# A dense layer's first matrix by one level of Strassen, its activations through DRAM

## Chip, cores and metric

The kernel runs on one core of a Trainium2 chip. The metric is the device time of one launch in microseconds (us), lower is better; it is given as the median of three runs. The trace is that of one profiled execution.

## What is computed

Attention between 8 batches of rows and 32 state rows, a top-1 mixture of 8 experts over the 4352 resulting rows of 512 features, and a dense layer over the same rows. The change lies in the dense layer, the last third of the reference:

```python
def _moe2_ref(x, w_in, w_out):          # x 4352 x 512, w_in 512 x 2048, w_out 2048 x 512
    h = x @ w_in
    beta = 1.0
    neg = h <= -beta
    pos = h >= beta
    g = np.where(pos, h, np.where(neg, 0.0, (h + beta) ** 2 / (4.0 * beta)))
    return (g @ w_out).astype(np.float32)
```

The mixture hands its rows over as y, still without each row's scale (gate weight times output gate): x = scale * y.

## The kernel before

The kernel has one core's engines: TensorE (PE) for matrix products, VectorE (DVE), ScalarE (ACT), Pool for element-wise work and indirect DMAs, and SP, whose queue issues most DMAs. Everything up to the dense layer takes the first 597 us of the trace and stays as it is. One program is written and a scheduler sets each engine's order from it; buffers come from pools of a fixed number, and the tools put in the waits.

**Three passes.** A float32 operand is held as h, its rounding to the 12-bit format float32r, and l, the rest (a cast on ScalarE, a subtraction on VectorE); a product is h·h + l·h + h·l, three matmuls of the fast format that add up in one PSUM bank.

**The dense layer.** The 34 tiles of 128 tokens are worked in blocks: tiles 0 and 1, then seven blocks of four tiles, then two of two (`blocks`, L393). For a block `dense_in` (L395) loads y, transposed, in 512 x 512 (features by tokens), multiplies it by the scale (DVE, L411) and splits it (ACT L412, DVE L413). The 2048 hidden features are 16 chunks of 128. The weights of a chunk, its 512 x 128 of w_in and its 128 x 512 of w_out in one tile of 1024 columns, are split in the first block (`split_w`, L167 to L171) and stay in 32 tiles. `ff_l1` (L418) makes one chunk of h for a block: 12 matmuls (4 blocks of 128 features x 3 passes, L427) with as many columns as the block has tokens, 512 or 256. Then the function g is made of h in four steps, and the result is split for the next product (ACT L440, DVE L441):

```python
V.tensor_scalar(c[:, 0:n], p[:, 0:n], 1.0, -1.0, op0=ALU.min, op1=ALU.max)      # L434
A.activation(r[:, 0:n], p[:, 0:n], AF.Relu, bias=neg1)                          # L435
A.activation(c[:, 0:n], c[:, 0:n], AF.Square, bias=half, scale=0.5)             # L436
V.tensor_add(c[:, 0:n], c[:, 0:n], r[:, 0:n])                                   # L437
```

`ff_l2` (L461) takes a chunk of g as the stationary operand: for each tile of the block 3 matmuls of 512 columns (L470) that add to that tile's output bank; after 16 chunks `store_z` (L450) copies the bank out (ACT L453) and writes the rows to their places (Pool, indirect DMA, L454). The schedule (L1193 on) goes through all (block, chunk) steps and runs the second matrix two steps (`AHEAD`) behind the first, across the borders of blocks. So TensorE alternates between 12 matmuls of a first and of a second matrix. g never leaves the core's memory.

PSUM is cut into eight banks of 512 columns: two (`ptp`) for transposes, two (`pl1`) for h, four (`pacc`) for outputs. The pool `np_` belongs to a preparation of the weights that is over before the dense layer; `gp` has six tiles of 512 columns for short-lived values.

Of the kernel before, what the change touches and what calls it, by code (L numbers as in the profile page):

```python
# [1277 lines left out]
```

## Time and profile before

| | us |
|---|---|
| runs | 1353.61, 1356.83, 1357.52 |
| median | 1356.83 |
| span of the profiled execution | 1351.2 |
| of it up to the dense layer's first product | 597.5 |
| dense layer, block 0 (2 tiles) | 44 |
| dense layer, seven blocks of 4 tiles | 616 |
| dense layer, two blocks of 2 tiles | 87 |
| from the last product to the end | 7 |

The rows to read are those of the engines in the dense layer: how long each is busy in a stretch, how far apart TensorE's matmuls start, and how long one operation of each kind takes on VectorE, ScalarE and Pool. A matmul's own duration in the trace is longer than its place in the pipeline, since matmuls overlap; the distance between starts is what counts. PEclk is the share of full clock that TensorE was granted.

### The profile page before, as it was taken

To read this page: it belongs to the slowest core of one execution; us is meant where nothing else is said; L and a number is where in the kernel's file an instruction comes from. 1 tells how busy PE (TensorE), PEld (TensorE's weight loads), DVE (VectorE), ACT (ScalarE), POOL (GpSimd) and SP (SyncE) were. 2 spreads that over 40 slices of the span, in tenths; PEclk is the share of its full clock that TensorE was granted. 3 is DMA by queue.
4 is the path that set the end of the run, shared out by engine and by line. 5 is a ranking of instruction groups with operands and counts; after the bars stand their busy time and mean duration, and the time that the engine had idled before them with its cause. 6 is when DMAs were issued, how large, how long until landed. Compare 5 with 4: busy or idle time off the path is not lost.

```text
span 1351.2 us, 17570 instructions
## 1 busy us (share of the span) xinstructions
PE 1305.1 (97%) x6534; PEld 1081.3 (80%) x6534; DVE 706.5 (52%) x1303; ACT 579.6 (43%) x982; POOL 139.3 (10%) x146
## 2 busy tenths in 40 slices
PE   6988989989899999999999999999999999999997
PEld 3767778767887788899888888888888888888996
DVE  5787768756765535355453443534435344343443
ACT  3654256434543435355344334433344343433443
POOL 2212022122132001000001001000010010100100
PEclk8999989999999999999999999999999999999999
DMA  6976398867777546250000101001010010000100
GB/s 237 334 253 223 91 351 261 300 194 226 254 229 231 183 141 226 94 185 9 32 24 32 40 0 48 24 8 63 1 47 25 0 47 20 32 16 16 35 17 16
DMA packets 79043, 154.23 MB, mean 114 GB/s; under 512 B 12068, under 2 KB 35048, under 8 KB 78952
## 3 DMA queue, kind: packets, MB, share of 16 engines
q1 hardware_dynamic: 70952, 129.94, 29.1%
q0 software_dynamic: 8000, 23.11, 4.9%
q8 instruction: 53, 0.87, 0.3%
q14 instruction: 38, 0.31, 0.1%
HBM read 116.79 MB, written 36.23 MB: 113 GB/s over the span
## 4 chain that ended last, share of the span: by engine, by line
issue 61%; PE 16%; DMA 11%; DVE 5%; POOL 2%; ACT 2%; SPq 1%; POOLq 0%; ACTq 0%; DVEq 0%
DMA wf_dram<-n 7%; PE h L284 6%; PE y L345 4%; DMA raw<-w 3%; POOL out L454 2%; PE xp L1017 2%; PE sc L916 1%; PE sp L994 1%; DVE n L263 1%; DVE n L264 1%; PE xp L194 1%; SPq L248 1%; DMA xg<-x_dram,inv_i 1%; PE ip L614 0%; DVE n L257 0%
## 5 line engine op out<-in xcount | busy, mean ns | idle before, releaser
L435 ACT ACTIVATE cr<-fh,neg 128x512 f32<-128x512 f32 (+1 forms) x160 | 99.8, 624 | 303.5 <-DVE cr L434 303.5
L437 DVE TENSOR_TENSOR cr<-cr 128x512 f32<-128x512 f32 (+1 forms) x160 | 97.9, 612 | 182.5 <-ACT cr L436 182.5
L434 DVE TENSOR_SCALAR cr<-fh 128x512 f32<-128x512 f32 (+1 forms) x160 | 97.7, 610 | 137.3 <-PE fh L427 132.3
L441 DVE TENSOR_TENSOR gl<-cr,gh 128x512 fp32r<-128x512 f32 (+1 forms) x160 | 97.8, 611 | 96.3 <-ACT gh L440 95.7
L440 ACT CAST gh<-cr 128x512 fp32r<-128x512 f32 (+1 forms) x160 | 89.2, 557 | 108.9 <-DVE cr L437 107.8
L454 POOL DMA_INDIRECT out<-zs,row_i x34 | 33.4, 981 | 793.2 <-ACT zs L453 787.8
L436 ACT ACTIVATE cr<-cr,half 128x512 f32<-128x512 f32 (+1 forms) x160 | 103.7, 648 | 0.0
L256 ACT ACTIVATE n<-n 128x256 f32<-128x256 f32 x64 | 28.0, 437 | 103.8 <-DMA wf_dram<-n 99.8
L287 ACT ACTIVATE hh<-h 128x512 fp32r<-128x512 f32 (+2 forms) x96 | 48.4, 505 | 56.1 <-PE h L284 55.9
L288 DVE SCALAR_TENSOR_TENSOR hl<-h,hh 128x512 fp32r<-128x512 f32 (+2 forms) x96 | 55.1, 574 | 23.1 <-ACT hh L287 21.5
L176 POOL DMA_INDIRECT xg<-x_dram,inv_i x38 | 40.7, 1072 | 215.3 <-DMA yT_dram<-ys 83.8
L257 DVE TENSOR_SCALAR n<-n 128x256 f32<-128x256 f32 x64 | 18.9, 295 | 61.4 <-ACT n L256 49.1
L804 POOL DMA_INDIRECT ls_dram<-pk,cdest_i x34 | 38.1, 1119 | 109.1 <-DMA ls_dram<-pk,cdest_i 107.6
L1017 PE MATMUL xp<-sB_sb,at_sb 128*128 128x272 f32 x128 | 34.4, 417 | 3.0 <-ACT at_sb L983 2.3
L194 PE MATMUL xp<-ident,xg 128*128 128x128 f32 x144 | 22.9, 284 | 10.8 <-DMA xg<-x_dram,inv_i 6.8
L1017 PEld LDWEIGHTS xp<-sB_sb,at_sb 128*128 128x128 f32 x128 | 23.3, 195 | 10.5 <-ACT at_sb L983 2.7
L194 PEld LDWEIGHTS xp<-ident,xg 128*128 128x128 f32 x144 | 18.2, 146 | 16.3 <-issue 12.3
L345 PE MATMUL y<-hh,w_1h 128*128 128x512 f32 (+1 forms) x80 | 30.1, 376 | 0.6 <-ACT ys L310 0.5
L345 PE MATMUL y<-hh,w_7h 128*128 128x512 f32 (+1 forms) x80 | 29.8, 373 | 0.0
L345 PE MATMUL y<-hl,w_3h 128*128 128x512 f32 (+1 forms) x80 | 29.7, 371 | 0.0
L345 PE MATMUL y<-hh,w_3h 128*128 128x512 f32 (+1 forms) x80 | 29.6, 370 | 0.0
L345 PE MATMUL y<-hh,w_7l 128*128 128x512 f32 (+1 forms) x80 | 29.5, 369 | 0.0
(1642 smaller groups left out, 3794.6 us busy)
## 6 DMA issues: line engine op xcount, KB each, us to landing
raw<-w SPq DMA_DIRECT2D x80, 512.0 KB
n<-wio SPq DMA_DIRECT2D x64, 256.0 KB
yT_dram<-ys SPq DMA_DIRECT2D x36, 256.0 KB
fy<-yT_dram SPq DMA_DIRECT2D x17, 512.0 KB
xn<-xn SPq DMA_DIRECT2D x32, 260.0 KB
xT<-xT SPq DMA_DIRECT2D x32, 256.0 KB
x_dram<-xr SPq DMA_DIRECT2D x32, 256.0 KB
wf_dram<-n SPq DMA_DIRECT2D x64, 128.0 KB
```

The source lines that it names most:

```text
L194: PE.transpose(p[:, k], rows[:, k * 128:(k + 1) * 128], ident)
L284: PE.matmul(p[:, 0:n], a, b, start=(i == 0), stop=(i == len(prods) - 1))
L288: last["V"] = V.scalar_tensor_tensor(hl[:, 0:n], p[:, 0:n], 0.0, hh[:, 0:n].bitcast(F32), op0=ALU.max, op1=ALU.subtract)
L345: PE.matmul(yacc[s, k * n // KK][:, c:c + n * 128], w[:, o + k * 128:o + k * 128 + 128], h[:, 0:n * 128], **g)
L434: V.tensor_scalar(c[:, 0:n], p[:, 0:n], 1.0, -1.0, op0=ALU.min, op1=ALU.max)
L435: A.activation(r[:, 0:n], p[:, 0:n], AF.Relu, bias=neg1)
L436: A.activation(c[:, 0:n], c[:, 0:n], AF.Square, bias=half, scale=0.5)
L437: V.tensor_add(c[:, 0:n], c[:, 0:n], r[:, 0:n])
L440: A.copy(gh[:, 0:n], c[:, 0:n])
L441: V.tensor_sub(gl[:, 0:n], c[:, 0:n], gh[:, 0:n].bitcast(F32))
L454: z = G.indirect_dma_start(out=out, out_offset=bass.IndirectOffsetOnAxis(ap=row_i[:, t:t + 1], axis=0), in_=zs, in_offset=None,)
L1017: PE.matmul(xp[:, g, 0:272], at_sb[:, g, st * 128:(st + 1) * 128], sB_sb[:, b, g], start=True, stop=True,)
```

## The change

Block 0 (tiles 0 and 1) is worked as before, but for two things: its weights are split into one tile for w_in and one for w_out (each with h and l side by side, `split_ff`), and g is made by `bend`, one step of ScalarE and two of VectorE, as max(h, a · min(a, 1)) with a = relu((h + 1) / 2). 

For the other 32 tiles the first matrix is done by Strassen's scheme in the form of Winograd. A group p is 1024 tokens, cut in two halves of 512; a quad q is two chunks of 128 hidden features. With the depth of 512 cut in two halves as well, the quad's 2 x 2 outputs come from seven products of half depth (`PRODS`) in place of eight: each has two blocks of 128 features x 3 passes = 6 matmuls of 512 columns, 42 in a quad in place of 48. The operands are sums and differences: of x in `x_raw` and `x_split`, made once for a group (14 tiles of h and l), of w_in in `w_sums`, made once on Pool, split in the first group, stored to DRAM (`wv_dram`) and loaded again for the later groups (`w_next`). The products share three banks per quad (x, y from the pools `ptp`, `pl1`; z from `ptp`); a bank is read between products, and five sums and a copy on VectorE and ScalarE put the outputs together. `g_out` bends each of the four 128 x 512 pieces and stores it to DRAM, on SP's queue.

The second matrix for these tiles reads g back (`l2_load`, three buffers in the place of `np_`), splits it (`l2_split`) and runs per half group of four tiles as before. Its chunks are spent by a budget, 3.5 in a quad (`PER`) from the sixth quad on (`LAG`), 4 more at the end of a group (`GAP`), and what is left behind the last quad.

```diff
+    def split_ff(raw, nm):
+        got = []
+        for part, c in (("i", 0), ("o", 512)):
+            if part == "i":
+                wi_pools.append(wstate["n"] % NW)
+            t = w_tile(F32R, f"{nm}{part}").rearrange("p (a f) -> p a f", a=2)
+            A.copy(t[:, 0], raw[:, c:c + 512])
+            V.tensor_sub(t[:, 1], raw[:, c:c + 512], t[:, 0].bitcast(F32))
+            got.append(t)
+        return got
...
-    blocks = [(0, 2)] + [(2 + 4 * i, 4) for i in range(7)] + [(30, 2), (32, 2)]
+    blocks = [(0, 2)]
+    NPAIR = (NT - 2) // 8
...
+    def bend(h, a, out):
+        A.activation(a, h, AF.Relu, bias=half, scale=0.5)
+        V.scalar_tensor_tensor(a, a, 1.0, a, op0=ALU.min, op1=ALU.mult)
+        V.tensor_tensor(out, h, a, op=ALU.max)
...
-        V.tensor_scalar(c[:, 0:n], p[:, 0:n], 1.0, -1.0, op0=ALU.min, op1=ALU.max)
-        A.activation(r[:, 0:n], p[:, 0:n], AF.Relu, bias=neg1)
-        A.activation(c[:, 0:n], c[:, 0:n], AF.Square, bias=half, scale=0.5)
-        V.tensor_add(c[:, 0:n], c[:, 0:n], r[:, 0:n])
+        c = gp.tile([128, 512], F32, tag="g", name=f"cr{j}_{fc}")[:, 0:n]
+        bend(p[:, 0:n], c, c)
...
+    PRODS = [("11", "11"), ("S2", "T2"), ("S1", "T1"), ("12", "21"), ("S3", "T3"), ("22", "T4"), ("S4", "22")]
...
+    def x_raw(p):
+        t0 = 256 + 1024 * p
+        sv = late_tile(spool, ns_, f"sv{p}", F32)
+        SP.dma_start(
+            sv, s_dram.rearrange("(o t) p -> o (t p)", o=1)[:, t0:t0 + 1024].to_broadcast([128, 1024]),
+        )
+        got = []
+        for k in (0, 1):
+            raws = []
+            for kk in (k, k + 2):
+                r = raw_tile(f"xr{p}_{kk}")
+                SP.dma_start(r, yT_dram[:, kk, t0:t0 + 1024])
+                G.tensor_mul(r, r, sv)
+                raws.append(r)
+            b11, b12, b21, b22 = [r[:, c:c + 512] for r in raws for c in (0, 512)]
+            t3 = gp.tile([128, 512], F32, tag="g", name=f"t3_{p}_{k}")
+            V.tensor_sub(t3, b22, b12)
+            V.tensor_sub(b12, b12, b11)
+            got.append({"11": b11, "T2": b11, "21": b21, "T3": t3, "T1": b12, "T4": b21, "22": b22})
+        return got
+    def x_split(p, k, nm, got):
+        v = got[k][nm]
+        if nm == "T2":
+            V.tensor_add(v, got[k]["T3"], v)
+        elif nm == "T4":
+            V.tensor_sub(v, v, got[k]["T2"])
+        t = late_tile(xpool, nx_, f"X{p}_{nm}_{k}", F32R).rearrange("p (a f) -> p a f", a=2)
+        A.copy(t[:, 0], v)
+        V.tensor_sub(t[:, 1], v, t[:, 0].bitcast(F32))
+        X[p, nm, k] = t
...
+        raw, u = [raw_tile(nm) for nm in (f"wr{q}", f"ws{q}")]
+        for j in range(2):
+            SP.dma_start(raw[:, j * 512:j * 512 + 512], wf_dram[2 * q + j][:, 0:512])
+        a11, a12, a21, a22 = [raw[:, c:c + 256] for c in range(0, 1024, 256)]
+        s1, s2, s3, s4 = [u[:, c:c + 256] for c in range(0, 1024, 256)]
+        G.tensor_add(s1, a21, a22)
+        G.tensor_sub(s2, s1, a11)
+        G.tensor_sub(s3, a11, a21)
+        G.tensor_sub(s4, a12, s2)
+        wsum[q] = {"11": a11, "S2": s2, "12": a12, "S3": s3, "S1": s1, "22": a22, "S4": s4}
...
+    def w_next(p, q, i):
+        if q == NQ2:
+            p, q = p + 1, 0
+        if p == NPAIR:
+            return
+        nm, m, j = PRODS[i][0], q // 2, q % 2
+        if j == 0:
+            W[i] = late_tile(wpool, nw_, f"W{p}_{m}_{nm}", F32R)
+            if p:
+                SP.dma_start(W[i].bitcast(F32), wv_dram[m][i])
+        if p == 0:
+            w = W[i].rearrange("p (a j f) -> p a j f", a=2, j=2)
+            v = wsum[q][nm]
+            A.copy(w[:, 0, j], v)
+            V.tensor_sub(w[:, 1, j], v, w[:, 0, j].bitcast(F32))
+            if j:
+                SP.dma_start(wv_dram[m][i], W[i].bitcast(F32))
...
+        g = gip.tile([128, 512], F32, tag="r", name=f"gi{p}_{t}_{fc}")
+        SP.dma_start(g, g_dram[p, t, fc])
...
+        g = gin.pop(c)
+        gh = hp_.tile([128, 512], F32R, tag="gh", name=f"gh{p}_{t}_{fc}")
+        gl = hp_.tile([128, 512], F32R, tag="gl", name=f"gl{p}_{t}_{fc}")
+        A.copy(gh, g)
+        V.tensor_sub(gl, g, gh.bitcast(F32))
...
+    def l2():
+        c = done["mm"]
+        for what, ahead, f in (("load", 4, l2_load), ("split", 2, l2_split)):
+            while done[what] < min(c + ahead, len(chunks)):
+                f()
...
+    def product(p, q, i, bank, start):
+        nm = PRODS[i][1]
+        w = W[i].rearrange("p (a j k f) -> p a j k f", a=2, j=2, k=2)[:, :, q % 2]
+        n = 0
+        for k in range(2):
+            x = X[p, nm, k]
+            for a, b in ((0, 0), (1, 0), (0, 1)):
+                PE.matmul(
+                    bank, w[:, a, k], x[:, b], start=(start and n == 0), stop=(n == 5), skip_group_check=True,
+                )
+                n += 1
+    def g_out(p, q, r, c, h, a):
+        bend(h, a, a)
+        g_dram[p, c, 2 * q + r] = dram.tile([128, 512], F32, name=f"g{p}_{c}_{2 * q + r}")
+        SP.dma_start(g_dram[p, c, 2 * q + r], a)
...
+    def quad(p, q, hook, after):
+        x = ptp.tile([128, 512], F32, tag="tp", name=f"qx{p}_{q}")
+        product(p, q, 0, x, True)
+        after(0)
+        tu = late_tile(tpool, nt_, f"tu{p}_{q}", F32)
+        t, u2 = tu[:, 0:512], tu[:, 512:1024]
+        A.copy(t, x)
+        y = pl1.tile([128, 512], F32, tag="l1", name=f"qy{p}_{q}")
+        product(p, q, 1, y, True)
+        after(1)
+        V.tensor_add(u2, y, t)
+        z = ptp.tile([128, 512], F32, tag="tp", name=f"qz{p}_{q}")
+        product(p, q, 2, z, True)
+        after(2)
+        hook(0)
+        product(p, q, 3, x, False)
+        after(3)
+        g_out(p, q, 0, 0, x, a_tile(f"a11_{p}_{q}"))
+        product(p, q, 4, y, False)
+        after(4)
+        u3 = a_tile(f"u3_{p}_{q}")
+        V.tensor_add(u3, y, t)
+        hook(1)
+        product(p, q, 5, y, False)
+        after(5)
+        V.tensor_add(t, t, y)
+        V.tensor_add(u3, u3, z)
+        g_out(p, q, 1, 0, t, a_tile(f"a21_{p}_{q}"))
+        g_out(p, q, 1, 1, u3, a_tile(f"a22_{p}_{q}"))
+        hook(2)
+        product(p, q, 6, z, False)
+        after(6)
+        V.tensor_add(u2, u2, z)
+        g_out(p, q, 0, 1, u2, a_tile(f"a12_{p}_{q}"))
+        hook(3)
+        done["quad"] = p * NQ2 + q
+    LAG, PER, GAP = 5, 3.5, 4
+    budget = [0.0]
+    def spend():
+        while budget[0] >= 1 and done["mm"] < len(chunks):
+            budget[0] -= 1
+            l2()
+    w_sums(0)
+    for i in range(len(PRODS)):
+        w_next(0, 0, i)
+    vals = x_raw(0)
+    for _, nm in PRODS:
+        for k in range(2):
+            x_split(0, k, nm, vals)
+    for gq in range(NPAIR * NQ2):
+        p, q = divmod(gq, NQ2)
+        last = q == NQ2 - 1
+        if p == 0 and not last:
+            w_sums(q + 1)
+        if last and p + 1 < NPAIR:
+            vals = x_raw(p + 1)
+        def hook(n):
+            if gq >= LAG:
+                budget[0] += PER / 4
+                spend()
+        def after(i):
+            if q % 2 or p == 0:
+                w_next(p, q + 1, i)
+            if last and p + 1 < NPAIR:
+                for k in range(2):
+                    x_split(p + 1, k, PRODS[i][1], vals)
+        quad(p, q, hook, after)
+        if last:
+            budget[0] += GAP
+            spend()
+    while done["mm"] < len(chunks):
+        l2()
```

TensorE's order where block 0 ends. Before, the first chunk of the next block (fh1_0) stands between block 0's second-matrix chunks (f1h0 is the block's input, wff_0h the split weights):

```order
L470 MATMUL z0_0_7143<-wff_13h_7059,gh0_13_7459 128x512 [waits Activation_49]
L470 MATMUL z0_0_7143<-wff_13l_7060,gh0_13_7459 128x512
L470 MATMUL z0_0_7143<-wff_13h_7059,gl0_13_7460 128x512 [waits DVE_49]
L470 MATMUL z0_1_7147<-wff_13h_7059,gh0_13_7459 128x512
L470 MATMUL z0_1_7147<-wff_13l_7060,gh0_13_7459 128x512
L470 MATMUL z0_1_7147<-wff_13h_7059,gl0_13_7460 128x512
L427 MATMUL fh1_0_7525<-f1h0_7137,wff_0h_5349 128x512 [waits Activation_49]
L427 MATMUL fh1_0_7525<-f1h0_7137,wff_0l_5350 128x512
L427 MATMUL fh1_0_7525<-f1l0_7139,wff_0h_5349 128x512
L427 MATMUL fh1_0_7525<-f1h0_7137,wff_0h_5349 128x512
L427 MATMUL fh1_0_7525<-f1h0_7137,wff_0l_5350 128x512
```

After, the first quads stand there alone, behind the rest of block 0. The names: qx0_1 is bank x of group 0, quad 1; X0_T4_0 the operand T4 of group 0, feature block 0; W0_0_S3 the weight operand S3 of group 0 for quads 0 and 1; x3 stands for three matmuls:

```order
L1353 MATMUL qy0_0_7688<-X0_T3_0_7648,W0_0_S3_7593 128x512 [waits DVE_49]
L1353 MATMUL qy0_0_7688<-X0_T3_0_7648,W0_0_S3_7593 128x512 x2
L1353 MATMUL qy0_0_7688<-X0_T3_1_7651,W0_0_S3_7593 128x512 x3
L1353 MATMUL qx0_1_7782<-X0_11_0_7622,W0_0_11_7581 128x512 [waits DVE_49,Activation_49]
L1353 MATMUL qx0_1_7782<-X0_11_0_7622,W0_0_11_7581 128x512 x2
L1353 MATMUL qx0_1_7782<-X0_11_1_7625,W0_0_11_7581 128x512 x3
L1353 MATMUL qy0_1_7794<-X0_T2_0_7629,W0_0_S2_7584 128x512 [waits Activation_49]
L1353 MATMUL qy0_1_7794<-X0_T2_0_7629,W0_0_S2_7584 128x512 [waits DVE_49]
L1353 MATMUL qy0_0_7688<-X0_T4_0_7655,W0_0_22_7596 128x512 [waits DVE_49]
L1353 MATMUL qy0_0_7688<-X0_T4_0_7655,W0_0_22_7596 128x512 x2
L1353 MATMUL qy0_0_7688<-X0_T4_1_7659,W0_0_22_7596 128x512 x3
L1353 MATMUL qz0_0_7699<-X0_22_0_7662,W0_0_S4_7599 128x512 [waits DVE_49]
```

The second-matrix matmuls are gone from between the products; quad 1's first product has moved ahead of quad 0's sixth (T4), and each product waits for VectorE. The first second-matrix matmul of these tiles stands 115 matmuls behind the start of quad 0.

VectorE's order at the same place. Before, three steps in each chunk:

```order
L434 TENSOR_SCALAR cr0_15_7510<-fh0_15_7497 128x256 [waits PE_49]
L437 TENSOR_TENSOR cr0_15_7510<-cr0_15_7510 128x256 [waits Activation_49]
L441 TENSOR_TENSOR gl0_15_7516<-cr0_15_7510,gh0_15_7515 128x256 [waits Activation_49]
L434 TENSOR_SCALAR cr1_0_7538<-fh1_0_7525 128x512 [waits PE_49]
L437 TENSOR_TENSOR cr1_0_7538<-cr1_0_7538 128x512 [waits Activation_49]
L441 TENSOR_TENSOR gl1_0_7544<-cr1_0_7538,gh1_0_7543 128x512 [waits Activation_49]
L434 TENSOR_SCALAR cr1_1_7566<-fh1_1_7553 128x512 [waits PE_49]
L437 TENSOR_TENSOR cr1_1_7566<-cr1_1_7566 128x512 [waits Activation_49]
```

After, the rows behind block 0's last step; t3 and xr are sums of y times scale (L1240 to L1250), X the split operands (L1253), tu the sum of banks y and x (L1378):

```order
L1248 TENSOR_TENSOR xr0_1_7613<-t3_0_1_7619,xr0_1_7613 128x512 [waits DVE_49]
L1253 TENSOR_TENSOR X0_T3_0_7648<-t3_0_0_7610,X0_T3_0_7648 128x512 [waits Activation_49]
L1253 TENSOR_TENSOR X0_T2_0_7629<-xr0_0_7604,X0_T2_0_7629 128x512 [waits Activation_49]
L1253 TENSOR_TENSOR X0_T2_1_7633<-xr0_1_7613,X0_T2_1_7633 128x512 [waits Activation_49]
L1253 TENSOR_TENSOR X0_T1_0_7636<-xr0_0_7604,X0_T1_0_7636 128x512 [waits Activation_49]
L1253 TENSOR_TENSOR X0_T1_1_7639<-xr0_1_7613,X0_T1_1_7639 128x512 [waits Activation_49]
L1253 TENSOR_TENSOR X0_21_0_7642<-xr0_2_7607,X0_21_0_7642 128x512 [waits PE_49,Activation_49]
L1253 TENSOR_TENSOR X0_21_1_7645<-xr0_3_7616,X0_21_1_7645 128x512 [waits PE_49,Activation_49]
L1253 TENSOR_TENSOR X0_T3_1_7651<-t3_0_1_7619,X0_T3_1_7651 128x512
L1250 TENSOR_TENSOR xr0_2_7607<-xr0_2_7607,xr0_0_7604 128x512 [waits DVE_49]
L1250 TENSOR_TENSOR xr0_3_7616<-xr0_3_7616,xr0_1_7613 128x512 [waits DVE_49]
L1378 TENSOR_TENSOR tu0_0_7686<-qy0_0_7688,tu0_0_7686 128x512 [waits PE_49]
```

Where VectorE had three steps for each chunk, the sums and splits of the group's operands stand in a row, and the first sum of a bank stands behind them.

## Rows read from the trace of the kernel before

**Rows 1.** The page's first part: busy time, share and instructions of each engine.
```profile
PE 1305.1 (97%) x6534; PEld 1081.3 (80%) x6534; DVE 706.5 (52%) x1303; ACT 579.6 (43%) x982; POOL 139.3 (10%) x146
```

**Rows 2.** Windows: length; PE, PEld, DVE, ACT, POOL busy (instructions); clock, DMA share, GB/s.
```profile
641.45:1257.00 615.55, 615.55 (x2731) 510.27 (x2730) 263.90 (x370) 245.12 (x387) 26.55 (x27) 1.00 0.08 26
1257.00:1300.00 43.00, 43.00 (x278) 39.15 (x278) 20.95 (x47) 20.41 (x47) 2.92 (x3) 1.00 0.08 28
1300.00:1344.00 44.00, 44.00 (x273) 39.03 (x271) 19.25 (x46) 20.61 (x48) 1.97 (x3) 1.00 0.04 13
```

**Rows 3.** Timeline of TensorE in a four-tile block: start, duration, line, operation.
```profile
1182.72 0.39 PE L427 MATMUL fh<-f7h,wff_4h 128*128 128x512 f32 x1
...
1188.16 0.39 PE L427 MATMUL fh<-f7h,wff_5h 128*128 128x512 f32 x1
```

**Rows 4.** Timeline of TensorE in the last two-tile block.
```profile
1338.14 0.28 PE L427 MATMUL fh<-f9h,wff_15h 128*128 128x256 f32 x1
...
1339.58 0.40 PE L470 MATMUL z<-wff_13h,gh 128*128 128x512 f32 x1
```

**Rows 5.** Lines by form, 650 to 1200 us: busy, mean ns | idle before, releaser.
```profile
L437 DVE TENSOR_TENSOR cr<-cr 128x512 f32<-128x512 f32 x102 | 70.5, 692 | 130.8 <-ACT cr L436 130.8
...
L436 ACT ACTIVATE cr<-cr,half 128x512 f32<-128x512 f32 x102 | 72.6, 712 | 0.0
...
L440 ACT CAST gh<-cr 128x512 fp32r<-128x512 f32 x102 | 63.4, 622 | 77.1 <-DVE cr L437 77.1
```

**Rows 6.** Timeline of VectorE and ScalarE: operations in a row, and block 0's.
```profile
592.71 1.22 DVE L171 TENSOR_TENSOR wff_13l<-rawff,wff_13h 128x1024 fp32r<-128x1024 f32 x1
593.85 1.22 DVE L171 TENSOR_TENSOR wff_14l<-rawff,wff_14h 128x1024 fp32r<-128x1024 f32 x1
...
304.22 0.43 DVE L263 SCALAR_TENSOR_TENSOR n<-n,n 128x256 int32<-128x256 int32 x1
304.68 0.43 DVE L264 SCALAR_TENSOR_TENSOR n<-n,n 128x256 int32<-128x256 int32 x1
...
619.09 0.47 ACT L435 ACTIVATE cr<-fh,neg 128x256 f32<-128x256 f32 x1 [0.82 <-DVE cr L434]
...
620.51 0.41 ACT L440 CAST gh<-cr 128x256 fp32r<-128x256 f32 x1 [0.55 <-PE fh L427]
...
620.95 0.42 DVE L441 TENSOR_TENSOR gl<-cr,gh 128x256 fp32r<-128x256 f32 x1 [0.53 <-ACT gh L440]
```

**Rows 7.** Start of block 0: timeline of TensorE, then a window.
```profile
597.47 0.36 PE L427 MATMUL fh<-f0h,wff_0h 128*128 128x256 f32 x1 [2.06 <-PEq L1183]
...
599.07 0.42 PE L427 MATMUL fh<-f0h,wff_1h 128*128 128x256 f32 x1
599.29 0.41 PE L427 MATMUL fh<-f0h,wff_1l 128*128 128x256 f32 x1
...
598.80:602.20 3.40, 3.40 (x18) 3.35 (x17) 0.66 (x2) 0.87 (x2) 0.00 (x0) 0.50 0.13 25
```

**Rows 8.** Timeline: a store and its reader's wait; a load and its reader's wait.
```profile
300.89 0.43 SPq L268 DMA_DIRECT2D wf_dram<-n  x1
...
303.10 0.43 ACT L256 ACTIVATE n<-n 128x256 f32<-128x256 f32 x1 [4.22 <-DMA wf_dram<-n]
...
581.21 0.61 SPq L409 DMA_DIRECT2D fy<-yT_dram  x1
...
585.44 1.22 DVE L411 TENSOR_TENSOR fy<-fy,fs 128x1024 f32<-128x1024 f32 x1 [1.95 <-issue]
```

**Rows 9.** Timeline of the end: the copy behind the last matmul.
```profile
1344.05 0.58 ACT L453 COPY zs<-z 128x512 f32<-128x512 f32 x1 [0.34 <-PE z L470]
```

**Rows 10.** Timeline in the attention, VectorE and Pool; then Pool by line.
```profile
64.15 1.24 DVE L1005 TENSOR_TENSOR sr<-sp,r 32x128 f32<-32x128 f32 x4
64.26 1.91 POOL L972 TENSOR_TENSOR e<-e,rs 128x1024 f32<-128x1024 f32 x1 [8.18 <-DVE r L1002]
...
L801 POOL COPY pk<-cst_sb 128x34 f32<-128x34 f32 x1 | 0.2, 227 | 0.0
```

More of the change, by code (lines that the diff above doesn't have):

```diff
@@ L1180, in fused_kernel @@
     manual.close()
+    np_ctx.close()
     def extras(i):
@@ L1190, in fused_kernel @@
     extras(0)
-    fsteps = [(j, fc) for j in range(len(blocks)) for fc in range(FC2)]
-    fgen, fpend = None, {}
-    for i in range(len(fsteps) + AHEAD):
-        if i < len(fsteps):
-            j, fc = fsteps[i]
-            if j == 0:
-                stream.need(("ff", fc))
-                stream.step(1.0)
-                stream.load()
-            fpend[i] = ff_l1(j, fc)
-            if fc == 2 and j + 1 < len(blocks):
-                fgen = dense_in(j + 1)
-                fx[j + 1] = next(fgen)
-        if i >= AHEAD:
-            j2, fc2 = fsteps[i - AHEAD]
-            if j2 == len(blocks) - 1 and fc2 == FC2 - 2:
-                held = (fc2, *fpend.pop(i - AHEAD))
-            elif j2 == len(blocks) - 1 and fc2 == FC2 - 1:
-                ff_l2(j2, [held, (fc2, *fpend.pop(i - AHEAD))])
-            else:
-                ff_l2(j2, [(fc2, *fpend.pop(i - AHEAD))])
-        if i < len(fsteps) and fgen is not None and fc >= 6:
-            next(fgen, None)
+    NQ2 = FC2 // 2
@@ new lines, in fused_kernel, with late_tile, wi_pool @@
+    xpool, wpool, tpool, spool = [], [], [], []
+    def late_tile(pools, state, nm, dt):
+        pool_, tag = pools[state[0] % len(pools)]
+        state[0] += 1
+        return pool_.tile([128, 1024], dt, tag=tag, name=nm)
+    nx_, nw_, nt_, ns_ = [0], [0], [0], [0]
+    gip = pool("gip", 3)
+    X, W = {}, {}
+    PRODS = [("11", "11"), ("S2", "T2"), ("S1", "T1"), ("12", "21"), ("S3", "T3"), ("22", "T4"), ("S4", "22")]
+    def wi_pool(i):
+        return wp0 if i < NW0 else wp1 if i < NW1 else wstate["late"]
@@ new lines, in x_split @@
+    def x_split(p, k, nm, got):
[8 more added lines that the diff above has]
+        X[p, nm, k] = t
+    wv_dram = [
+        [dram.tile([128, 1024], F32, name=f"wv{m}_{a}") for a, _ in PRODS] for m in range(NQ2 // 2)
+    ]
@@ new lines, in fused_kernel @@
+    fpend = {}
+    for i in range(FC2 + AHEAD):
+        if i < FC2:
+            stream.need(("ff", i))
+            stream.step(1.0)
+            stream.load()
+            fpend[i] = ff_l1(0, i)
+        if i >= AHEAD:
+            ff_l2(0, 2, [(i - AHEAD, *fpend.pop(i - AHEAD))])
+    own = [(wi_pool(i), "w") for i in wi_pools]
+    xpool += [(xtp, "x")] * 8 + own[0:6]
+    wpool += own[6:13]
+    tpool += own[13:15]
+    spool += own[15:16]
+    chunks = [(p, t, fc) for p in range(NPAIR) for t in range(2) for fc in range(FC2)]
@@ new lines, in fused_kernel, with l2_load, l2_split @@
+    g_dram, gin, gsp = {}, {}, {}
+    done = {"load": 0, "split": 0, "mm": 0, "quad": -1}
+    def l2_load():
+        c = done["load"]
+        p, t, fc = chunks[c]
+        assert p * NQ2 + fc // 2 <= done["quad"], (c, done)
+        g = gip.tile([128, 512], F32, tag="r", name=f"gi{p}_{t}_{fc}")
+        SP.dma_start(g, g_dram[p, t, fc])
+        gin[c] = g
+        done["load"] += 1
+    def l2_split():
+        c = done["split"]
+        p, t, fc = chunks[c]
+        g = gin.pop(c)
[3 more added lines that the diff above has]
+        V.tensor_sub(gl, g, gh.bitcast(F32))
+        gsp[c] = (fc, gh, gl)
+        done["split"] += 1
@@ new lines, in l2 @@
+    def l2():
[3 more added lines that the diff above has]
+                f()
+        p, t, fc = chunks[c]
+        t0 = 2 + 8 * p + 4 * t
+        done["mm"] += 1
+        if c == len(chunks) - 2:
+            return
+        ff_l2(t0, 4, [gsp.pop(c - 1), gsp.pop(c)] if c == len(chunks) - 1 else [gsp.pop(c)])
+    def product(p, q, i, bank, start):
[9 more added lines that the diff above has]
+                n += 1
```

45 lines of the change are left out of this document (21 added, 24 removed).

## Prediction

> **What bounds the kernel now.** I read the engine shares first, then the dense layer in windows. TensorE is busy 1305.1 of 1351.2 us, 97%; VectorE 52%, ScalarE 43% [rows 1]. In the dense layer that is sharper: from the start of the four-tile blocks to their end TensorE is busy 615.55 of 615.55 us at a granted clock of 1.00, and so it is in the two two-tile blocks behind them, while VectorE is busy 263.90 us and ScalarE 245.12 us of those 615.55 [rows 2]. So nothing waits there but for TensorE, and a matrix product less is its own time less, until another engine becomes late. The span is 1351.2 us; the runs took 1353.61 to 1357.52, so the median, 1356.83, lies 5.6 us above the span. I forecast the span and add 5.6.
>
> **What is removed.** A chunk of a four-tile block is 12 matmuls of the first matrix and 12 of the second, all of 512 columns: the 24 that begin at 1182.72 last until the next chunk begins at 1188.16, 5.44 us / 24 = 226.7 ns each [rows 3]. A chunk of a two-tile block has 12 of 256 columns: 1338.14 to 1339.58, 1.44 us, 120 ns each [rows 4]. First matrix for tiles 2 to 33 before: 7 blocks x 16 chunks x 12 = 1344 matmuls of 226.7 ns = 304.7 us, and 2 x 16 x 12 = 384 of 120 ns = 46.1 us. After: 4 groups of 1024 tokens x 8 quads x 7 products x 6 = 1344 matmuls of 512 columns, 304.7 us (the order of the changed kernel shows this number). The second matrix stays at 1536 matmuls of 512 columns, block 0 as it was. The gain on TensorE is therefore **46.1 us**: an eighth of the first matrix, 43.5, and the 2.6 by which those 384 cost over half of 512 columns.
>
> **What is added, and what hides it in the steady part.** A quad yields 2 x 2 pieces of 128 features by 512 tokens. On VectorE it takes 5 additions, 4 x 2 operations of the new bend and 4 subtractions that split the reloaded pieces: 17 of 512 columns. Such an operation is shown with 692 ns [rows 5], but operations that don't depend on each other overlap a little at their ends (592.71, 593.85: 1.14 us apart at 1.22 us each), and dependent ones stand 0.03 apart (304.22, 304.68) [rows 6]. So 0.61 to 0.73 each; I take 0.65 where operations of both kinds mix, 11.1 us in a quad, and 0.63 where most are independent. ScalarE: a copy, 4 bends and 4 casts, 9 by 0.62 to 0.71 = 6 us. TensorE has 42 + 3.5 x 12 = 84 matmuls in a quad, 19.0 us. Both engines have room, and the order puts 12 matmuls of the second matrix (2.7 us) between a product and the next use of its bank. I cost the 28 or so steady quads at nothing; what covers them is those 84 matmuls.
>
> **The first three quads are not covered.** Behind block 0 there is no second-matrix work yet (LAG = 5), and VectorE works off in its order what the first products need: 3 steps of block 0's last chunk, 6 sums, 8 splits of the operands X, 2 more sums, and so on. Say E is the end of block 0's last first-matrix matmul. VectorE is through with that chunk at E + 2.2 us (at 256 columns ScalarE's Relu 0.47 and cast 0.41, three operations of VectorE at 0.42 [rows 6]). Then come 19 operations of 512 columns, 19 x 0.63 = 12.0, and two of the bend, five of 256 columns at 0.36 and the u3 sum, 3.7: u3 is done at E + 17.9. TensorE has 56 matmuls till then, 18 of block 0 and 38 of the products: 12.7 us. So the first quad alone waits some 5.2 us. Up to the last sum of quad 2, VectorE has 54 operations of 512 and 21 of 256 columns: 2.2 + 54 x 0.63 + 21 x 0.36 = 43.8 us; TensorE has 158 matmuls, 35.8 us. That is a floor of 8.0 us; following the hand-overs one by one I get 10 to 11, and with 0.69 and 0.42 for each operation 14.8. I take **11**.
>
> **The clock.** A gap costs more than itself: after 2.06 us without a matmul the first chunk of block 0 began at full clock, and then the granted clock fell to 0.50, the lower of the two levels (1.2 for 2.4 GHz), for 3.40 us; 18 matmuls started there, 0.22 us apart (599.07, 599.29) where 0.12 is the pace [rows 4, 7]. 3.40 us at half speed is 1.7 us lost. The changed kernel has several gaps of 1 us and more in its first three quads; I take two such dips, **3.4** (0 to 7).
>
> **Quads 3 to 6** of the first group still split and store the weight operands (7 splits of 256 columns in a quad) with thin second-matrix filling: VectorE has 57 operations of 512 and 28 of 256 columns, 46.0 us, to TensorE's 227 matmuls, 51.5 us. At 89% hand-overs show: **4** (1 to 8), a quarter to one us a quad and twice that at worst. **Group changes:** 14 operand tiles are made anew while the last quad runs, and the order fills with second-matrix chunks; 2.5 for the first, with the weight splits beside it, 1.0 for the two others: **3.5** (1 to 7).
>
> **DRAM round trip of g.** 256 KB pieces are stored and loaded on SP's queue. A store of 128 KB was seen by its reader 2.2 us after its issue (300.89 to 303.10), a load of 512 KB was usable at the latest 4.2 us after its issue (581.21 to 585.44) [rows 8]. The load is issued four chunks ahead and the split two ahead, two to four times 2.72 us: hidden, 0. If that cover goes, it costs each of 128 chunks (rival 3). The **tail** keeps its form, a copy of 0.58 us behind the last matmul and an indirect store [rows 9]: 0.
>
> **Sum.** 1351.2 - 46.1 + 11 + 3.4 + 4 + 3.5 = 1327.0 us of span, + 5.6 = **1333 us** (1.8% less than 1356.83). With all lower ends (8.0, 0, 1, 1) it is 1321, with all upper ones (14.8, 7, 8, 7) 1348; they will not all fall together, so 1326 to 1341 is this case's own range.
>
> **Rivals.**
> 1. *Pool and VectorE get in each other's way.* The W sums of the first group (4 of 256 columns in a quad) and the product of X with its scale (4 of 1024 columns in a group) run on Pool, in the stretch in which VectorE is the late engine. A 1024-column product took 1.91 us on Pool, a copy of 34 columns 0.23 us [rows 10], so 256 columns are 0.6 us by interpolation. Beside that 1.91 us VectorE ran four of its own (64.15 for 1.24 us), but those read one operand from PSUM [rows 10]; no row has an operation of VectorE with two SBUF operands beside one of Pool. If these block each other for their whole length: 7 quads x 4 x 0.6 = 16.8 us, three quarters of them exposed, 12.6, and half of the 7.6 us of one group's X products where its first change is bare, 3.8: 16.4 more, 1349. For it: nearly all of VectorE's added work there has two SBUF operands. Against: it counts only where VectorE sets the end. The row above, with one SBUF operand and no delay, agrees with one half of what the Trainium skill says (SBUF — State Buffer, Who interferes with whom): a VectorE instruction with at most one SBUF input does not contend with GpSimd. Its other half, that one with two SBUF inputs contends with a GpSimd instruction that reads SBUF, over a lock held for the whole instruction, no row here shows; by it the sum is this rival's 1349, without it 1333.
> 2. *Better cover.* The scheduler's order lets TensorE go on with the next quad's products while sums are late, and the dips don't come: floor 8.0 alone plus 3 for the rest: 1351.2 - 46.1 + 11.0 + 5.6 = 1322 (1317 to 1326).
> 3. *The other side: the round trip is not hidden.* All stores of g, loads of g, weight loads and weight stores stand in one queue on SP; a store that waits for its bend holds up the loads behind it. Of the gain 24 us are left; they are gone when each of the 128 chunks waits 0.19 us, and the kernel is slower by more than the 0.3% (4.1 us) that a measurement of it can tell from no change when each waits 0.22 us. At 0.35 us, which is 5% of the 7.7 us of store, load, cast and subtraction, it is 1333 + 45 = 1378. For it: 64 MB more on one queue. Against: DMA is busy 0.08 in this stretch [rows 2], and the chunks lead by 5 to 11 us.
> 4. *It does not do what it says:* half-depth products with other operands run slower than 226.7 ns. Weight and column shapes are the same, so little for it.
>
> **How the numbers follow.** Forecast 0.52 (1326 to 1341), rival 1 0.24 (1342 to 1356), rival 2 0.14, rival 3 and 4 0.10 (above 1356). Under 1352.8, faster by over 0.3%, are the first, rival 2 and 0.7 of rival 1: 0.83; the rest of rival 1 and a little of rival 3 are within: 0.07; 0.10 slower. The range leaves out 0.1 above and about 0.06 below: 1318 to 1355.
>
> **What would show it.** Right: 1344 product matmuls at 226.7 ns, TensorE gapless in the groups 1 to 3, and 10 to 20 us of idle TensorE within 90 us behind block 0, released by VectorE, with a clock of 0.50 behind gaps. Rival 1: VectorE operations of over 1 us beside Pool's sums. Rival 3: TensorE or ScalarE waiting for loads of g in the groups 1 to 3. Wrong altogether if TensorE idles evenly over all quads: then it is a hand-over in every quad that I cost at nothing.

## The result: slower by 1.1%, where 1.8% faster was forecast

| | before | after |
|---|---|---|
| median of the runs, us | 1355.22 | 1371.38 |
| lowest and highest, us | 1353.05, 1357.52 | 1365.87, 1373.13 |
| span of the profiled execution, us | 1351.2 | 1369.9 |

The ratio is 1.0113, 95% interval 1.0082 to 1.0144: the whole interval lies above 1, so the kernel is slower. (The kernel before has one run more here than in its table above, so its median moved from 1356.83 to 1355.22.) 1371 lies 38 us over the forecast and outside its range. In spans the miss is larger, 1369.9 for 1327.0 or 42.9 us: the 5.6 us that the forecast added between span and median were 1.5 here.

The page of the changed kernel, first part (busy time, share of the span, instructions), answers to [rows 1]:

```profile
PE 1286.3 (94%) x6150; PEld 1039.1 (76%) x6150; DVE 850.3 (62%) x1543; ACT 537.0 (39%) x934; POOL 210.4 (15%) x193
```

TensorE has less to do (its busy time fell from 1305.1 to 1286.3 us), and over the whole kernel it is idle 83.6 us in place of 46.1. Where, the windows tell. They are cut at block 0, the end of quad 2, of quad 6, of the next group's quad 0 (the first group change), of the last quad before the second change, and behind that change. The columns are those of [rows 2]: length, then PE, PEld, DVE, ACT, POOL busy (instructions), clock, DMA share, GB/s.

```profile
600.01:650.57 50.56, 44.99 (x271) 40.43 (x271) 24.90 (x53) 16.42 (x40) 10.96 (x6) 0.94 0.17 54
655.34:704.77 49.43, 37.87 (x141) 27.09 (x140) 43.80 (x73) 22.81 (x49) 13.90 (x14) 0.93 0.66 242
704.77:765.02 60.25, 53.75 (x229) 42.13 (x227) 48.91 (x85) 25.47 (x55) 13.76 (x16) 1.00 0.71 262
765.02:833.69 68.67, 56.82 (x222) 45.08 (x221) 49.94 (x65) 23.81 (x41) 25.42 (x12) 0.90 0.65 231
833.69:966.48 132.79, 132.79 (x580) 108.49 (x578) 82.45 (x130) 45.71 (x74) 3.88 (x4) 1.00 0.63 216
966.48:1000.57 34.09, 31.89 (x137) 25.29 (x136) 25.00 (x30) 12.23 (x21) 14.62 (x8) 1.00 0.69 231
1000.57:1363.10 362.53, 362.53 (x1579) 295.85 (x1577) 191.89 (x298) 115.27 (x185) 17.93 (x19) 1.00 0.54 182
```

For block 0 the same stretch of the kernel before was 42.62 us, without idle time:

```profile
597.47:640.09 42.62, 42.62 (x271) 39.23 (x272) 22.45 (x50) 20.82 (x47) 0.00 (x0) 0.96 0.13 43
```

The loss of a stretch is its length less its matmuls at 226.7 ns each; their numbers, for the six windows from quad 0 on, are 140, 227, 221, 578, 136 and 1578. The forecast had charged this:

| stretch | forecast, us | loss, us |
|---|---|---|
| dense layer begins later (597.47, now 600.01) | 0 | 2.5 |
| block 0 | 0 | 7.9 |
| quads 0 to 2 | 11 + 3.4 for the clock | 17.7 |
| quads 3 to 6 | 4 | 8.8 |
| first group change (quad 7 and the next quad 0) | 2.5 | 18.6 |
| second and third group change | 1.0 | 3.8 |
| other quads and the rest of the second matrix | 0 | 6.1 |
| between block 0's last first-matrix product and quad 0 | 0 | 0.7 |

Block 0 is taken against the 42.62 us. The sum is 66.1 us; the kernel before lost 0.8 us by the same measure, and the tail is 0.4 shorter, so 66.1 - 46.1 - 1.2 = 18.8 us, and the spans differ by 18.7. In the steady quads nothing waits, as forecast: between 833.69 and 966.48 TensorE is busy all the time at full clock, and from 1000.57 on too. They lose 6.1 us all the same, since the matmuls stand further apart: 132.79 us for 578 are 229.7 ns each. The rest of the loss lies in block 0, in the first group and in the first two changes, and in each of these windows Pool is busy with 11 to 25 us.

**What stands in them.** First block 0: Pool's X product, then rows of ScalarE, VectorE and TensorE at the same time (start, duration, line; in brackets idle time and releaser).

```profile
612.98 0.62 ACT L1252 CAST X<-xr 128x512 fp32r<-128x512 f32 x1 [4.73 <-POOL xr L1236]
612.91 2.36 POOL L1236 TENSOR_TENSOR xr<-xr,sv 128x1024 f32<-128x1024 f32 x1
613.63 2.18 DVE L1253 TENSOR_TENSOR X<-xr,X 128x512 fp32r<-128x512 f32 x1 [4.55 <-ACT X L1252]
613.96 0.73 PE L482 MATMUL z<-wff_2o,gh 128*128 128x512 f32 x2 [0.87 <-ACT gh L455]
615.73 0.41 DVE L456 TENSOR_TENSOR gl<-cr,gh 128x256 fp32r<-128x256 f32 x1
616.20 0.50 PE L482 MATMUL z<-wff_2o,gl 128*128 128x512 f32 x1 [1.51 <-DVE gl L456]
```

A subtraction of 512 columns, 0.69 us in [rows 5], takes 2.18: it ends 0.54 us after Pool's operation (612.91 + 2.36 = 615.27). The next operation is the split of g for which TensorE waits 1.51 us. ScalarE is held as well: a cast of X stands 4.73 us for Pool's product, with the cast of g behind it for which TensorE waits 0.87. Of block 0's 5.57 us without a matmul (50.56 - 44.99) these two and one like them, 1.92 us at 649.03, make 4.30. The remaining 1.27, at 605.76, lies ahead of Pool's first X product and is a wait for VectorE's bend. Next the first group change:

```profile
775.55 0.62 ACT L1252 CAST X<-xr 128x512 fp32r<-128x512 f32 x1 [5.37 <-POOL xr L1236]
776.08 0.58 ACT L1374 COPY tu<-qx 128x512 f32<-128x512 f32 x1
...
777.84 2.82 POOL L1236 TENSOR_TENSOR xr<-xr,sv 128x1024 f32<-128x1024 f32 x1
778.36 2.85 DVE L1240 TENSOR_TENSOR t<-xr,xr 128x512 f32<-128x512 f32 x1
780.62 2.79 POOL L1236 TENSOR_TENSOR xr<-xr,sv 128x1024 f32<-128x1024 f32 x1
781.24 2.71 DVE L1241 TENSOR_TENSOR xr<-xr 128x512 f32<-128x512 f32 x1
783.87 0.68 DVE L1378 TENSOR_TENSOR tu<-qy,tu 128x512 f32<-128x512 f32 x1
784.61 0.79 PE L1353 MATMUL qy<-X_T,W_S 128*128 128x512 f32 x1 [5.15 <-DVE tu L1378]
```

Two things are seen. Pool and VectorE take turns, one whole operation each. And what they do is not urgent: it belongs to the next group, but stands in the queues ahead of the copy and the sum (L1374, L1378) for which TensorE waits 5.15 us. Two more gaps of that window, 2.10 and 4.60 us, end with VectorE too. The three are 11.9 of the 18.6 us; the rest goes with the lower clock (0.90). Where VectorE reads one operand from PSUM, it is not held up, though Pool works on:

```profile
825.12 2.85 POOL L1236 TENSOR_TENSOR xr<-xr,sv 128x1024 f32<-128x1024 f32 x1
825.64 0.68 DVE L1389 TENSOR_TENSOR u<-qy,tu 128x512 f32<-128x512 f32 x1
826.36 0.69 DVE L1394 TENSOR_TENSOR u<-u,qz 128x512 f32<-128x512 f32 x1
```

Taken over the dense layer, VectorE's operations beside one of Pool's are 30.0 us longer than the median of their kind; the others, taken together, are not longer.

### The profile page after: what moved, and what is told of

Same layout as the page of the kernel before. It is cut to its first block, busy times and chain, and to the rows that moved or that the text cites. A ratio compares the mean times of both kernels' runs of the same rounds, so it can differ in the third digit from the quotient of the medians.

```text
span 1369.9 us, 18187 instructions
## 1 busy us (share of the span) xinstructions
PE 1286.3 (94%) x6150; PEld 1039.1 (76%) x6150; DVE 850.3 (62%) x1543; ACT 537.0 (39%) x934; POOL 210.4 (15%) x193
## 4 chain that ended last, share of the span: by engine, by line
PE 35%; issue 9%; DVE 6%; DMA 3%; POOL 1%; ACT 1%; SPq 0%; POOLq 0%; DVEq 0%; ACTq 0%
PE z L482 18%; PE qy L1353 7%; PE qz L1353 5%; PE qx L1353 4%; DMA wr<-wf_dram 1%; DVE a L437 1%; DVE a L438 1%; DVE X L1253 1%; PE fh L449 1%; DVE gl L1330 1%; POOL out L466 1%; DMA xr<-yT_dram 1%; DVE X_T L1253 0%; DMA gi<-g 0%; POOL xr L1236 0%
## 5 line engine op out<-in xcount | busy, mean ns | idle before, releaser
L1330 DVE TENSOR_TENSOR gl<-gi,gh 128x512 fp32r<-128x512 f32 x128 | 95.7, 750 | 128.8 <-ACT gh L1329 128.7
L1329 ACT CAST gh<-gi 128x512 fp32r<-128x512 f32 x128 | 79.5, 622 | 226.9 <-PE z L482 179.4
L437 DVE SCALAR_TENSOR_TENSOR a<-a 128x512 f32<-128x512 f32 x128 | 90.2, 725 | 71.6 <-ACT a L436 70.0
L1353 PE MATMUL qy<-X_T,W_S 128*128 128x512 f32 x384 | 104.1, 403 | 13.9 <-DVE tu L1378 8.3
L1353 PE MATMUL qx<-X,W 128*128 128x512 f32 x384 | 99.2, 391 | 6.1 <-DVE a L438 6.1
L1353 PEld LDWEIGHTS qy<-X_T,W_S 128*128 128x128 f32 x384 | 73.0, 192 | 33.9 <-DVE tu L1378 10.0
L1353 PEld LDWEIGHTS qx<-X,W 128*128 128x128 f32 x384 | 71.9, 188 | 23.1 <-ACT W_S L1288 3.8
L271 DVE TENSOR_SCALAR n<-n 128x256 f32<-128x256 f32 x64 | 18.7, 293 | 62.4 <-ACT n L270 55.0
L1353 PE MATMUL qz<-X_T,W_S 128*128 128x512 f32 x192 | 50.9, 399 | 3.1 <-DVE tu L1400 2.8
L1353 PE MATMUL qy<-X_T,W 128*128 128x512 f32 x192 | 51.6, 405 | 2.2 <-DVE u L1389 2.1
L1353 PE MATMUL qz<-X,W_S 128*128 128x512 f32 x192 | 49.3, 392 | 0.0
```

What stands on the lines that cost most here:

```text
L437: V.scalar_tensor_tensor(a, a, 1.0, a, op0=ALU.min, op1=ALU.mult)
L1329: A.copy(gh, g)
L1330: V.tensor_sub(gl, g, gh.bitcast(F32))
L1353: PE.matmul(bank, w[:, a, k], x[:, b], start=(start and n == 0), stop=(n == 5), skip_group_check=True,)
```

## Experiments

**Theory A:** Pool's X products and W sums and VectorE's operations with two operands in SBUF block each other. **Theory B:** VectorE's own load and the hand-overs do it, and Pool's share is a help. Three runs move work from Pool to VectorE, one leaves it out.

Both moved (`e1_on_dve`):

```diff
-                G.tensor_mul(r, r, sv)
+                V.tensor_mul(r, r, sv)
...
-        G.tensor_add(s1, a21, a22)
+        V.tensor_add(s1, a21, a22)
...
```

> The X products with the scale (16 of 1024 columns) and the W sums (32 of 256 columns) are made by VectorE in place of Pool; all else stays. Theory A, Pool and VectorE block each other: in the trace of the changed kernel VectorE's operations beside Pool's are longer by 30 us in sum; that goes, 16 x 1.14 + 32 x 0.36 = 30 us of VectorE's own work comes, but each operation is half as long as on Pool and most of the new work lies in block 0 and in covered quads. 1350 to 1358. Theory B, VectorE is late through its own work and the hand-overs, and Pool's help is worth having: 12 to 15 us slower, about 1384.

1352.39 us, ratio to the kernel before 0.9965 (0.9945 to 0.9985): 19 us less than the changed kernel, though VectorE has 30 us more of its own to do. Theory B falls. Quads 0 to 2 and the first change:

```profile
656.13:709.38 53.25, 39.00 (x143) 29.42 (x142) 42.08 (x86) 22.82 (x50) 2.77 (x2) 0.87 0.64 237
764.85:818.58 53.73, 52.44 (x223) 41.11 (x222) 45.59 (x69) 23.55 (x40) 4.31 (x4) 1.00 0.82 288
```

The first change loses 3.4 us in place of 18.6 (222 matmuls), block 0 5.0 in place of 7.9 and quads 3 to 6 4.7 in place of 8.8. Quads 0 to 2 lose more, 21.1 in place of 17.7 (142 matmuls).

X products alone (`e2_x_dve`, the first pair of lines):

> Only the X products with the scale move from Pool to VectorE; the W sums stay on Pool. Theory A: block 0 gets back most of its 8 us and the first group change some 5, so 1357 to 1362. Theory B: 5 us slower, about 1376.

1357.59 us, 1.0023 (0.9998 to 1.0048).

W sums alone (`e3_w_dve`, the other four):

> Only the W sums move from Pool to VectorE; the X products stay on Pool. Theory A: 28 sums in the first group block 0.55 us of VectorE each and take 0.36 there: 2 to 6 us faster, 1365 to 1369. Theory B: 10 us of more work where VectorE is late, about 1380.

1365.07 us, 1.0070 (1.0044 to 1.0097). The two parts, 13.8 and 6.3 us, add up to about the 19 of both.

No reading by Pool at all (`e4_no_pool`):

```diff
-        sv = late_tile(spool, ns_, f"sv{p}", F32)
...
-                G.tensor_mul(r, r, sv)
...
-        G.tensor_add(s1, a21, a22)
-        G.tensor_sub(s2, s1, a11)
-        G.tensor_sub(s3, a11, a21)
-        G.tensor_sub(s4, a12, s2)
+        G.memset(u, 0.5)
```

> Left out: the product of X with its scale (X is used as loaded, the scale row is not loaded), and the W sums, in whose place Pool fills the sums' tile with a constant (a write without a read). Theory A: VectorE's operations are nowhere over 0.70 us, block 0 takes 42 to 43 us, the first three quads lose 11 to 12 us in place of 18, quads 3 to 6 about 4 in place of 9: 1340 to 1348. Theory B: only Pool's latency at the group changes goes, 1362 to 1368.

1330.05 us, 0.9820 (0.9776 to 0.9865), 41 us less than the changed kernel and 10 below the range of Theory A. Its windows, block 0, quads 0 to 2, 3 to 6 and the first change:

```profile
599.35:643.29 43.94, 42.85 (x271) 39.16 (x272) 23.13 (x56) 17.15 (x41) 0.00 (x0) 0.96 0.16 50
647.46:687.80 40.34, 34.25 (x139) 24.78 (x137) 36.96 (x71) 22.09 (x49) 7.54 (x7) 1.00 0.74 275
687.80:741.18 53.38, 53.37 (x231) 42.72 (x229) 47.06 (x90) 26.22 (x56) 1.92 (x2) 1.00 0.87 320
741.18:791.24 50.06, 50.06 (x219) 40.74 (x218) 38.02 (x62) 23.61 (x40) 3.89 (x4) 1.00 0.84 292
```

I had set the first three quads at 11 to 12 us, quads 3 to 6 at 4; they lose 9.3 and 1.5, and the first change 0.7. Block 0 keeps 1.3 of its 7.9. Beside Pool's fill, which only writes, VectorE's operations with two SBUF operands keep their time (the first row is two operations):

```profile
657.85 0.75 DVE L1281 TENSOR_TENSOR W_S<-ws,W_S 128x256 fp32r<-128x256 f32 x2
658.04 0.95 POOL L1263 MEMSET ws<- 128x1024 f32 x1 [1.14 <-DVE X_T L1248]
658.52 0.68 DVE L437 SCALAR_TENSOR_TENSOR a<-a 128x512 f32<-128x512 f32 x1
```

So it is Pool's reading that blocks. What the Trainium skill says in SBUF — State Buffer, Who interferes with whom, is borne out in all three parts: two SBUF inputs against a reading Pool exclude each other for a whole instruction (778.36), one input does not (825.64), and a write alone does not (658.04). The 9.3 us of the first three quads (137 matmuls, 31.1 us, of 40.34) lie between the forecast's floor of 8.0 and the 11 that it took.

But the run with both moved to VectorE is 22 us above this one, and I read its added 30 us of VectorE as a part of that only: its quads 0 to 2 lose 21 us, more than the changed kernel's. Its rows at the end of quad 1:

```profile
678.57 0.72 ACT L436 ACTIVATE a<-tu,half 128x512 f32<-128x512 f32 x1
682.61 1.37 SPq L1265 DMA_DIRECT2D wr<-wf_dram  x2
687.58 0.40 ACT L1288 CAST W<-wr 128x256 fp32r<-128x256 f32 x1 [8.28 <-DMA wr<-wf_dram]
687.89 0.58 ACT L1374 COPY tu<-qx 128x512 f32<-128x512 f32 x1
688.52 0.80 PE L1353 MATMUL qx<-X,W 128*128 128x512 f32 x1 [8.31 <-ACT tu L1374]
```

ScalarE stands 8.28 us at a cast for a later quad, whose load was issued at 682.61 only; behind the cast in its queue waits the copy of bank x. The load came late since the four raw tiles (`rawp`) hold X until it is split, and W's raw values and sums want two of them per quad. **Theory C:** this costs by itself. **Theory D:** VectorE's own work sets the end there. The test gives W of quads 1 and 2 tiles of pools that stand idle at that time (`e5_tiles`, on top of both moved):

```diff
-        raw, u = [raw_tile(nm) for nm in (f"wr{q}", f"ws{q}")]
+        if q == 1:
+            r0, r1, u0 = [gip.tile([128, 512], F32, tag="r", name=f"{nm}{q}") for nm in ("wra", "wrb", "wsa")]
+            u1 = gp.tile([128, 512], F32, tag="g", name=f"wsb{q}")
+        elif q == 2:
+            r0, u0 = [hp_.tile([128, 512], F32, tag="gh", name=f"{nm}{q}") for nm in ("wra", "wsa")]
+            r1, u1 = [hp_.tile([128, 512], F32, tag="gl", name=f"{nm}{q}") for nm in ("wrb", "wsb")]
+        else:
+            raw, u = [raw_tile(nm) for nm in (f"wr{q}", f"ws{q}")]
...
```

> VectorE makes the X products and W sums, as in the run that moved both; besides, the loaded weights and sums of quads 1 and 2 get tiles of other pools that stand idle there (the three of the g loads and one short-lived one for quad 1, the split tiles of g for quad 2), so that their loads need not wait for the four raw tiles that hold X. Theory C, quad 1 of that run lost 11 us because the weights of quad 2 were loaded late and ScalarE stood 8.3 us at a cast for them: quads 0 to 2 lose 11 to 13 us in place of 21, 1341 to 1346. Theory D, VectorE's own work sets the end there: 1350 to 1353.

1335.52 us, 0.9876 (0.9847 to 0.9905). Quads 0 to 2, 3 to 6 and the first change:

```profile
647.40:687.59 40.19, 34.95 (x144) 26.13 (x143) 38.59 (x77) 21.06 (x45) 2.78 (x2) 1.00 0.56 205
687.59:743.79 56.20, 53.24 (x225) 41.21 (x223) 53.58 (x106) 25.91 (x54) 0.00 (x0) 1.00 0.81 294
743.79:797.57 53.78, 52.33 (x223) 41.17 (x222) 45.69 (x69) 23.53 (x40) 3.88 (x4) 1.00 0.83 288
```

The first three quads lose 7.8 us (143 matmuls, 32.4, of 40.19), quads 3 to 6 lose 5.6, the change 3.5; with 1.2 for the two other changes that is 18.1, to the 21.9 of the forecast. C holds, and it brought more than I expected: of the 13.3 us less in quads 0 to 2, 9.0 are idle time of TensorE and the rest goes with the clock (granted clock 1.00 here, 0.87 in that window with the raw tiles as changed). The scheduler also places the operations anew when the tiles change, so what the tiles give and what the new order gives is not separated.

The same tiles, with Pool's work left on Pool (`e7_tiles_pool`):

> The changed kernel with X products and W sums on Pool as it is, but with the other tiles for quads 1 and 2. If late weight loads cost by themselves, quad 2's 7.6 us shrink by 4 to 5: 1365 to 1368. If Pool beside VectorE sets that stretch: 1370 to 1373.

1351.67 us, 0.9966 (0.9938 to 0.9994): 20 us less, where I had expected 3 to 6; its runs scatter widely, from 1341.66 to 1358.84, and the profiled one took 1357.02. So the two causes are of one size and nearly add up (19.0 and 19.7 apart, 35.9 together):

| us | raw tiles as changed | other tiles |
|---|---|---|
| X products and W sums on Pool | 1371.4 | 1351.7 |
| on VectorE | 1352.4 | 1335.5 |

Counted from the dense layer's first product to the end, by the profiles, the four are 769.9 and 751.9, 747.6 and 733.7 us, to 753.7 before the change, so the differing starts of the dense layer do not make these differences. They are not two independent causes, though. The run without Pool's reading has the raw tiles as changed and loses only 10.8 us in quads 0 to 6: there the weight loads of quads 1 and 2 (told apart by their count) go out together, 7.9 us behind quad 0's start, where with both moved quad 2's go out 26.5 us behind it. I read this so that a load is late by as long as the work on X and W holds the tiles; that is argued, not tested.

My estimate for this run took in quads 0 to 6 alone: by its profile they lose 18.5 in place of 26.5, and the first group change loses 8.8 in place of 18.6. There the next group's first load of X goes out 21.6 us ahead of the change, in the changed kernel 3.7 us behind its start (768.75), which fits raw tiles that come free sooner; no run tests it by itself. What is left there is the 5 us gap of 784.61, here once more behind VectorE's operations of 2.7 to 2.9 us:

```profile
774.42 2.93 PE L1361 MATMUL qy<-X_T,W_S 128*128 128x512 f32 x6 [5.33 <-DVE tu L1386]
```

Is the product saved worth its time at all? On the run with both moved, the seventh product is made twice (`e6_eighth`; the sums are then not the layer's):

```diff
         product(p, q, 6, z, False)
+        product(p, q, 6, z, False)
```

> On the run that moved both to VectorE; the seventh product of each quad is made twice, so that there are eight products of 6 matmuls in a quad (the sums are not those of the layer). 192 matmuls of 226.7 ns are 43.5 us. If the matrix product saved is worth its time, all of it comes back outside the 9 quads that wait anyway: 1352 + 33 to 43.5 = 1385 to 1396. If something else sets the pace in the steady quads (VectorE, the round trip through DRAM): under 1375.

1387.77 us, 35.4 more. The matmul count rises by 192:

```profile
PE 1322.7 (95%) x6342; PEld 1074.4 (78%) x6342; DVE 852.4 (61%) x1591; ACT 538.0 (39%) x934; POOL 141.3 (10%) x145
```

In the first seven quads of group 1 behind its quad 0 the time rises from 132.79 to 143.22 us and the matmuls from 578 to 624 (42 added ones and 4 of the second matrix), 227 ns each. Of the 8 us that are missing to 43.5 most are waits of the first group that the added matmuls fill: by the profiles its quads and the first change lose 7.0 us less. The gain is real and its size was right.

Last, cover for quads 3 to 6 (`e8_lag`, on the run with the other tiles):

```diff
-    LAG, PER, GAP = 5, 3.5, 4
+    LAG, PER, GAP = 3, 3.5, 4
...
-                budget[0] += PER / 4
+                budget[0] += (2.0 if p == 0 else PER) / 4
```

> The run with VectorE's sums and the other tiles, with the second matrix begun in quad 3 at 2 chunks a quad in the first group (LAG 3, PER 2.0) in place of quad 5 at 3.5. Its chunks are 12 matmuls (2.72 us) for one operation of VectorE, so they cover hand-overs where VectorE is late. If the 5.6 us of quads 3 to 6 there are hand-overs without cover: 2 to 4 us less, 1332 to 1334 beside 1335.5. If they come from VectorE's own work: no change, and the first group change loses its cover: 1335 to 1338.

1333.52 us, 0.9829 (0.9797 to 0.9862): by its profile quads 3 to 6 lose 3.1 in place of 5.6 and the change 0.9 in place of 3.5. The totals of this and of `e5_tiles` (1335.52) are too near to tell apart; both are faster than the kernel before and than the changed one.

## Why the prediction was wrong

The gain was right: 1344 product matmuls, 46.1 us (the eighth product costs 35.4 us when it is put back, and its full 227 ns a matmul in the steady quads). So was the round trip through DRAM: from 1000.57 to the last product TensorE has no idle time in which it could show. The steady quads wait for nothing, as I had it, but at 229.7 ns a matmul for 226.7 they cost 6.1 us where I put nothing; that is a small form of rival 4, and its cause is open. The floor for the first quads was of the right size: without Pool's reading, or with it moved and the loads early, they lose 7.8 to 9.3 us, for a floor of 8.0 and 11 taken.

With both causes removed the kernel takes 1333.5 to 1335.5, close to the 1333 of the forecast, and that closeness is partly luck: `e5_tiles` loses 18.1 us where 21.9 were charged, but also 3.3 in block 0 and some 6 in the steady quads, where nothing was.

Three steps failed.

1. **Rival 1 was the case, and I gave it 0.24.** In the forecast itself Pool beside VectorE cost nothing. The rival's total was near, 16.4 us priced to 19.0 measured by moving Pool's work and 16.2 with the other tiles, but by luck, since its parts were wrong. I had 12.6 us from the W sums in quads 0 to 6 and 3.8 from the X products in half of one change; moved alone, the W sums gave 6.3 and the X products 13.8. The place was wrong too: moving both gave back 15.2 us at the first change and nearly nothing, 0.7, in quads 0 to 6. And block 0, which I had taken as it was, lost 7.9 us, of which 6.6 are gone without Pool's reading: there casts and subtractions of X, held up by Pool's products, stand ahead of the casts and splits of g. My one row for it [rows 10] showed Pool beside operations with one operand in PSUM, and that is no evidence for the ones that were added; the rows that would decide were absent, and absent rows count for neither side.
2. **Group changes, 2.5 us for the first, measured 18.6.** This is the largest single miss. I counted the 14 operands and forgot where they stand. They are written into the last quad's queues, and ScalarE and VectorE work in order: a cast that waits 5.37 us for Pool holds the copy of bank x behind it (775.55, 776.08). The order printed above for the end of block 0 shows the pattern, with L1253 and L1250 ahead of L1378. Position alone costs little: with the X products and W sums on VectorE the change loses 3.4 us. It was costly where these operations waited for Pool, and Pool (773.12) for a load of X that was issued at 768.75 only.
3. **The loads of W, no term at all.** I priced the first quads by VectorE's operations and assumed that their data are there. The four raw tiles serve X, W's raw values and W's sums at once; a tile that comes free late means a load issued late (680.57 in the changed kernel), then a wait of one engine in front of everything behind it. Other tiles for quads 1 and 2 gave 17 to 20 us, with the new order that came with them.

The clock term held in kind and was too small. Before the gap of 5.2 us the granted clock is 1.00, behind it 0.58 over 3.41 us, most of them at the lower level of 1.2 GHz:

```profile
777.90:779.40 1.50, 1.50 (x7) 0.94 (x6) 1.50 (x2) 0.00 (x0) 1.50 (x1) 1.00 1.00 407
779.40:784.60 5.20, 0.06 (x1) 0.00 (x0) 5.17 (x4) 0.62 (x1) 4.00 (x2) 0.95 0.79 321
784.61:788.02 3.41, 3.41 (x9) 2.74 (x10) 3.41 (x6) 2.23 (x4) 0.00 (x0) 0.58 0.00 0
```

Two dips were forecast; the windows with a clock under 1.00 are three (block 0, quads 0 to 2, the first change), and 0.07 of 49.43 and 0.10 of 68.67 us are about 3.5 and 6.9 us at most. The 3.4 us charged cover the first of these; the dips at the change came with its gaps.

What stays open: the dense layer began at 597.3 to 605.6 us in these runs, and at 597.47 in the kernel before, though nothing ahead of it was meant to change. Part is seen (a gap of 3.3 to 3.5 us at its start in place of 2.06 [rows 7]); the rest I did not trace. Every edit also gives the scheduler a new order of the operations, and no run holds the order fixed. Nor was it tried whether another order alone, with X and W on Pool, would do without the gap at the group change.
